# Eight PSUM banks as eight tiles instead of four pairs, in an attention and gated-product kernel on one core

## The chip, the cores and the metric

The kernel runs on one core of one Trainium2 chip. The metric is the device time of one execution in microseconds; lower is better. Three runs of the kernel before took 1008.64, 1010.52 and 1010.98 us, so the median is 1010.52 us.

## The reference

Windowed attention for 8 batches, 8 heads, 576 positions and head size 64 (four heads with a plain window of 32, four with a dilated one), and then a gated product on its output, all in float32:

```python
scores = scale * np.matmul(q, k.transpose(0, 1, 3, 2))
...
masks = np.stack([mask_plain if h < H // 2 else mask_dil for h in range(H)], axis=0)
scores = np.where(masks[None, :, :, :], scores, -1000000000.0)
scores = scores - np.max(scores, axis=-1, keepdims=True)
attn = np.exp(scores)
attn = attn / (np.sum(attn, axis=-1, keepdims=True) + 1e-09)
return np.matmul(attn, v).astype(np.float32)
...
g = x @ w_gate                      # x: 4608 x 512, w_gate and w_val: 512 x 1536
silu = g * (1.0 / (1.0 + np.exp(-g)))
val = x @ w_val
return (silu * val @ w_out).astype(np.float32)     # w_out: 1536 x 512
```

## The kernel before

The tokens are handled in nine chunks of 512. Attention is cut into "packs" of block-diagonal windows. For each pack TensorE writes scores into PSUM, VectorE subtracts the maximum, ScalarE takes the exponential, TensorE turns the result round and multiplies it by the values, and VectorE divides. Each float32 product of the second half is made of three matmuls of split operands (high by high, high by low, low by high), 128x512 each. The work comes in three stages.

**First packs.** Packs 0 to 3 run before any product, by an order written out by hand for TensorE, VectorE and ScalarE (the string of letters: Q scores, S shift, X exponential, T turn, K copy of the turned block, A results, N norm, G the first gate and value products, W stages that prepare weights).

**Plain chunks** (lines 880 to 912). Three chunks, twelve steps each, 36 steps s in all. A step makes twelve matmuls for the gate half g(s) into `bank_g` and twelve for the value half v(s) into `bank_v` (both line 485), and twelve output matmuls out(s-1) for the step before into the four banks `bank_o` (line 532). ScalarE takes the tanh of `bank_g` (line 504), VectorE multiplies it by `bank_g` (u, line 509) and by `bank_v` (h, line 514); ScalarE and GpSimd split h into high and low (lines 519 and 524), which out(s) reads. In program order a step is: g, tanh, u, v, h, out of the step before. VectorE also mixes weights for the third stage here (lines 696 to 709), and SyncE's queue writes them to memory as "pieces".

**Fast chunks** (lines 917 to 952). Three times two chunks at once, with seven products t = 0 to 6 in place of eight. In the gate part, for i = 0 to 5 and each t, `gate_val` makes six matmuls for r = 0 (gate) and six for r = 1 (value) (line 819). In the output part, for each t and i, `outs` makes three matmuls for r = 0 and three for r = 1. `BANK` says which pair of banks a t writes: 0 is `bank_g` and `bank_v`, 1 and 2 are the two pairs of `bank_o`; r picks the bank in the pair. After r = 0 or r = 1 of t = 0, 2 and 4 `keep` copies that bank to SBUF on ScalarE (line 824); after t = 1, 4, 5 and 6 `total` adds a bank and a kept copy on VectorE (line 780), in the gate part for both r after both products, in the output part (`out_done`) for each r right after its own product. Later products of the same pair add onto the bank, or start it afresh where t is in `FRESH`:

```python
BANK = (0, 1, 0, 2, 0, 1, 2)
FRESH = (0, 1, 3, 5)
KEPT = {0: 0, 2: 1, 4: 2}
SUMS = {1: ((0, 0), 1, 0), 4: ((1, 1), 2, 2), 5: ((1, 0), 1, 2), 6: ((0, 1), 2, 1)}
```

The weights' pieces come in through a ring of seven, each transfer asked for on GpSimd's queue (line 747) once TensorE has finished the piece whose place it takes.

PSUM has eight banks. Before, they are four tiles of two banks: `bgv` (gate and value), `two` (attention), `boa` and `bob` (outputs). The scores of the first packs use `bgv` and `boa`, their turned blocks the two halves of `bob`. Outside the hand-written part the order on each engine is set by a scheduler from the waits between tiles and its own estimate of durations; the waits themselves are put in by the framework from what each instruction reads and writes.

Of the kernel before, what the change touches and what calls it, by code (L numbers as in the profile page):

```python
# [10 lines left out]
F32 = mybir.dt.float32  # L11
# [7 lines left out]
P = 128  # L19
# [40 lines left out]
T0 = NPLAIN * CH  # L60
# [75 lines left out]
def attention_moe(ctx, tc, qkb, vb, w, const, out):  # L136
# [3 lines left out]
    def pk(m):  # L140
        return PACKS[m]
# [156 lines left out]
    def w_one(c):  # L298
        u = done[c]
        done[c] += 1  # L300
        if c == "E":
            w_exp(u)
        elif c == "T":
            w_shift(u)
        elif c == "B":
            w_bits(u)
        elif c == "H":
            w_split_hi(u)
        else:
            w_split_lo(u)  # L310
        if c in "BL":
            while ready["w"] and w_load():
                pass
# [22 lines left out]
    def load_qk(m, pool, engine, parts=1):  # L336
        t = pool["qk"]()
        n = pk(m).cols // parts
        for k in range(parts):
            engine.dma_start(out=t[:, n * k:n * k + n], in_=qkb[m, :, n * k:n * k + n])  # L340
        st[m]["qk"] = t
# [14 lines left out]
    def scores(m, two, masked):  # L356

        t = st[m]["qk"]
        if masked:
            for i in range(2):  # L360
                nc.tensor.matmul(out=two[:, i, SA:].rearrange("q (g k) -> q g k", g=NG), lhsT=ident16,
                                 rhs=masks_of(m, i), start=True, stop=False, skip_group_check=True)
        for g in range(NG):
            for j in range(NH):
                for i in range(2):
                    r, q, k = slice(D * i, D * i + D), pk(m).q_at(g, j), pk(m).k_at(i, g, j)
                    nc.tensor.matmul(out=two[BQ * j:BQ * j + BQ, i, SA + BU * g:SA + BU * g + BU],  # L367
                                     lhsT=t[r, q:q + BQ], rhs=t[r, k + 1:k + BK], start=not masked,
                                     stop=not masked or g == NG - 1, skip_group_check=True)

    def clear_e(pool):

        for a in pool["e"].starts:
            nc.gpsimd.memset(at(a, TP).rearrange("q (n k) -> q n k", k=BK)[:, :, :1], 0.0)

    def shift(m, two, pool, masked):
        mx = pool["bm"](2 * NG).rearrange("q (i g) -> q i g", i=2)
        e = pool["e"]()
        ev = e.rearrange("q (g i k) -> q i g k", g=NG, i=2)[:, :, :, 1:]
        s = two[:, :, SA:].rearrange("q i (g k) -> q i g k", g=NG)  # L380
        if not masked:
            n = BK * pk(m).mask
            if pk(m).mask_step:
                mk = mask_sb[:, n:n + 2 * BK * NG].rearrange("q (i g k) -> q i g k", i=2, g=NG)[:, :, :, 1:]
            else:
                mk = masks_of(m, 0).unsqueeze(1).broadcast_to([P, 2, NG, BU])
            nc.vector.tensor_tensor(out=ev, in0=s, in1=mk, op=ALU.add)
            s = ev
        nc.vector.reduce_max(out=mx, in_=s, axis=mybir.AxisListType.X)
        nc.vector.tensor_tensor(out=ev, in0=s, in1=mx.unsqueeze(3).broadcast_to([P, 2, NG, BU]), op=ALU.subtract)  # L390
        st[m]["e"] = e
# [5 lines left out]
    def turn_e(m, bank):  # L397
        for g in range(NG):
            nc.tensor.transpose(out=bank[:, P * g:P * g + P], in_=st[m]["e"][:, P * g:P * g + P], identity=eye)

    def keys(m, bank, pool):
        t = pool["pt"]()
        nc.scalar.copy(out=t, in_=bank)
        st[m]["pt"] = t

    def results(m, two):

        t, v = st[m]["pt"], st[m]["v"]
        for n in range(NH * NG):
            g, j = divmod(n, NH)  # L410
            for i in range(2):
                r = slice(D * i, D * i + D)
                nc.tensor.matmul(out=two[BQ * j:BQ * j + BQ, i, (D + 1) * g:(D + 1) * (g + 1)],
                                 lhsT=t[r, BQ * n:BQ * n + BQ], rhs=v[r, n, :], start=True, stop=True,
                                 skip_group_check=True)

    def norm(m, two, pool):
        z = pool["bz"](2 * NG).rearrange("q (i g) -> q i g", i=2)
        y = pool["y"]()
        s = two[:, :, :NG * (D + 1)].rearrange("q i (g c) -> q i g c", g=NG)  # L420
        nc.vector.tensor_scalar(out=z, in0=s[:, :, :, D], scalar1=EPS, scalar2=None, op0=ALU.add)
        nc.vector.reciprocal(out=z, in_=z)
        nc.vector.tensor_tensor(out=y.rearrange("q (c i g d) -> q i g c d", c=2, i=2, g=NG),  # L423
                                in0=s[:, :, :, :D].rearrange("q i g (c d) -> q i g c d", c=2),
                                in1=z.unsqueeze(3).unsqueeze(4).broadcast_to([P, 2, NG, 2, D // 2]), op=ALU.mult)
        st[m]["y"] = y
# [31 lines left out]
    def x_copy(m, what):  # L458
        src, xh, xl = x_views(m, *(t[pk(m).half % 2][pk(m).strided] for t in (x_hi, x_lo)))
        if what == "hi":  # L460
            nc.scalar.copy(out=xh, in_=src)
        else:
            nc.gpsimd.tensor_tensor(out=xl, in0=src, in1=xh, op=ALU.subtract)
# [17 lines left out]
    def gv_some(ci, f, which, ops, first, last):  # L481

        for n, (j, wl, xl) in enumerate(ops):
            o = 4 * P * (j // 2) + 2 * P * which + P * (j % 2)
            nc.tensor.matmul(out=(bank_g, bank_v)[which][:, :CH], lhsT=wcol(f, o, wl),  # L485
                             rhs=(x_lo if xl else x_hi)[ci % 2][1 - j // 2][:, j % 2],
                             start=first and n == 0, stop=last and n == len(ops) - 1)
# [3 lines left out]
    def gv_ops(text):  # L491

        return [(j, *PARTS[x]) for t in text.split() for x in t[1:] for j in ((2, 3) if t[0] == "p" else (0, 1))]
# [41 lines left out]
    def out_store(ci):  # L535
# [7 lines left out]


    fa = early
    bank_gv, two, bank_a, bank_b = [ctx.enter_context(tc.tile_pool(name="p" + x, bufs=1, space=bass.MemoryType.PSUM)).tile(
        [P, 2, 512], F32, name=x) for x in ("bgv", "two", "boa", "bob")]
    bank_g, bank_v = [bank_gv[:, n] for n in range(2)]
    bank_o = [x[:, n] for x in (bank_a, bank_b) for n in range(2)]
    s_banks, bank_r, k_bank = [bank_gv, bank_a], two, [bank_b[:, n % 2] for n in range(4)]  # L550

    nc.scalar.dma_start(out=const_sb, in_=const)
    load_qk(0, fa, nc.sync, 2)
# [28 lines left out]
    def more_in():  # L582
        load_v(3, fa, nc.sync, 2)
        w_load(2)
        w_load(2)
        w_load(2)
        ready["w"] = True
# [4 lines left out]
    first = {  # L592
        "Q": lambda m: scores(m, s_banks[m % 2], True), "S": lambda m: shift(m, s_banks[m % 2], fa, True),
        "X": exps, "T": lambda m: turn_e(m, k_bank[m]), "K": lambda m: keys(m, k_bank[m], fa),
        "A": lambda m: results(m, bank_r), "N": lambda m: norm(m, bank_r, fa),
        "U": turn_y, "H": lambda m: x_copy(m, "hi"), "L": lambda m: x_copy(m, "lo"),
        "M": lambda m: more_in(), "W": lambda n: w_one(STAGES[n]),
        "G": lambda n: gv_some(0, 0, first_gv[n][0], gv_ops(first_gv[n][1]), *first_gv[n][2:]),
    }

    et = mybir.EngineType
    with tc.manual_schedule(engines={et.PE, et.DVE, et.Activation}):
        for what in ("Q0 S0 Q1 X0 T0 S1 K0 X1 A0 M0 Q2 T1 K1 S2 N0 U0 X2 A1 W0 W1 W2 T2 K2 H0 L0 N1 W3 W4 U1 H1 L1 Q3 S3 A2 X3 N2 U2 "
                     "G0 W0 T3 K3 H2 L2 W1 W2 A3 W3 W4 N3 U3 G1 W0 W1 H3 L3 W2 G2 G3 G4 W3 G5 G6 W4 W0 W1 W2 W3 W4").split():
            first[what[0]](int(what[1]))
    load_qk(4, later, nc.sync)
    clear_e(later)
    while w_load():
# [252 lines left out]
    def n_out(ci, t, i):  # L861
        return NT * NP * ci + NP * t + i
# [54 lines left out]
    for ci in range(NC):  # L917
        base = SB + NSLOT * ci
        first = n_out(ci, 0, 0)
# [18 lines left out]
        for t in range(NT):  # L938
            for i in range(NP):
                n = n_out(ci, t, i)  # L940
# [57 lines left out]
```

## Time and profile before

| | |
|---|---|
| median of three runs | 1010.52 us |
| the profiled execution's own time | 1010.02 us |
| its span in the profile | 1008.2 us |
| TensorE (PE) busy | 940.2 us |
| weight loads (PEld) busy | 736.5 us |
| VectorE (DVE) busy | 663.4 us |
| ScalarE (ACT) busy | 391.0 us |
| GpSimd (POOL) busy | 363.6 us |
| mean granted TensorE clock | 0.977 |

The sum of a prediction is made against 1010.02 us, 1.8 us more than the span; the median of the runs is 0.5 us above that. In the rows, "PE" is a matmul, "PEld" the load of its weights; "idle before" or a bracket with an arrow names the work whose end released the instruction.

### The profile page before, as it was taken

The numbers are of one execution on the slowest core, as the hardware profiler recorded it, in microseconds if no ns is written. First come the engines' busy times: TensorE is split into PE (matmuls) and PEld (weight loads), VectorE is DVE, ScalarE is ACT, GpSimd is POOL, SyncE is SP. The second block draws the span as 40 slices with busy tenths as digits, with TensorE's granted clock in tenths as the row PEclk, the third lists the DMA queues.
The fourth block names the chain that finished last, engine by engine and source line by source line (L and its number), as shares of the span: only waits on it lengthen the run. The fifth ranks groups of instructions, "written<-read, shape, count | busy, mean of one in ns | idle before, by whom it ended". The sixth has DMA issues, their size and how long they took to land.

```text
span 1008.2 us, 20464 instructions
## 1 busy us (share of the span) xinstructions
PE 940.2 (93%) x8597; PEld 736.5 (73%) x8597; DVE 663.4 (66%) x966; ACT 391.0 (39%) x605; POOL 363.6 (36%) x369
## 2 busy tenths in 40 slices
PE   6799999999999999999999799999988999999988
PEld 3577776777777777777777587777766878877776
DVE  5466735676767786576679945767689745656933
ACT  3656532222233233333345343333344533333341
POOL 1555641212311221223334562232246733334562
PEclk7899999999999999999999899999999999999999
DMA  9556434565675792676685478777754676656562
GB/s 355 189 209 229 136 99 153 182 216 189 215 251 191 261 328 73 201 237 223 193 267 192 155 214 249 237 220 250 233 163 139 209 234 205 190 173 197 154 207 103
DMA packets 73964, 204.65 MB, mean 203 GB/s; under 512 B 7440, under 2 KB 21392, under 8 KB 73872
## 3 DMA queue, kind: packets, MB, share of 16 engines
q0 software_dynamic: 27216, 99.10, 32.4%
q1 hardware_dynamic: 36864, 66.43, 18.5%
q10 hardware_dynamic: 9792, 37.80, 11.1%
q8 instruction: 68, 1.11, 0.5%
q14 instruction: 24, 0.20, 0.1%
HBM read 160.84 MB, written 42.47 MB: 202 GB/s over the span
## 4 chain that ended last, share of the span: by engine, by line
PE 65%; DVE 23%; ACT 6%; issue 4%; DMA 1%; POOL 0%; ACTq 0%; SPq 0%; DVEq 0%
PE bgv L819 18%; PE bgv L485 14%; PE boa L819 12%; PE bob L819 12%; DVE at_float L780 5%; PE boa L532 3%; PE bob L532 3%; DVE at_float32r L780 2%; DVE at_float L847 2%; DVE at_float L848 1%; DVE at_float L509 1%; DVE at_float L423 1%; DVE at_float L696 1%; ACT at_float L504 1%; PE two L367 1%
## 5 line engine op out<-in xcount | busy, mean ns | idle before, releaser
L819 PE MATMUL bgv<-at_float32r 128*128 128x512 f32 x972 | 252.7, 400 | 14.1 <-ACT at_float L824 14.1
L485 PE MATMUL bgv<-at_float32r,at_float32r 128*128 128x512 f32 x864 | 222.1, 407 | 29.9 <-DVE at_float L509 17.8
L819 PEld LDWEIGHTS bgv<-at_float32r 128*128 128x128 f32 x972 | 178.6, 190 | 66.4 <-ACT at_float L824 30.7
L485 PEld LDWEIGHTS bgv<-at_float32r,at_float32r 128*128 128x128 f32 x864 | 162.1, 193 | 75.7 <-DVE at_float L509 26.7
L747 POOL DMA_DIRECT2D at_float32r<-pieces x189 | 103.2, 546 | 300.4 <-PE bgv L819 135.0
L819 PE MATMUL boa<-at_float32r 128*128 128x512 f32 x648 | 167.8, 399 | 10.4 <-DVE at_float L780 10.4
L819 PE MATMUL bob<-at_float32r 128*128 128x512 f32 x648 | 161.5, 394 | 1.3 <-DVE at_float L780 1.3
L819 PEld LDWEIGHTS boa<-at_float32r 128*128 128x128 f32 x648 | 123.3, 192 | 39.0 <-DVE at_float L780 12.5
L819 PEld LDWEIGHTS bob<-at_float32r 128*128 128x128 f32 x648 | 120.3, 188 | 29.1 <-DVE at_float L780 3.4
L780 DVE TENSOR_TENSOR at_float32r<-at_float,at_float32r 128x512 fp32r<-128x512 f32 (+1 forms) x84 | 88.2, 1058 | 55.8 <-ACT at_float32r L809 44.2
L524 POOL TENSOR_TENSOR at_float32r<-at_float,at_float32r 128x512 fp32r<-128x512 f32 x36 | 56.5, 1568 | 180.7 <-ACT at_float32r L519 87.9
L809 ACT CAST at_float32r<-at_float 128x512 fp32r<-128x512 f32 x126 | 76.2, 621 | 95.3 <-DVE at_float L780 27.4
L824 ACT COPY at_float<-bgv 128x512 f32<-128x512 f32 x126 | 73.9, 586 | 101.3 <-PE bgv L819 101.1
L780 POOL TENSOR_TENSOR at_float32r<-at_float,at_float32r 128x512 fp32r<-128x512 f32 x63 | 91.4, 1455 | 27.0 <-ACT at_float32r L809 26.2
L780 DVE TENSOR_TENSOR at_float<-bob,at_float 128x512 f32<-128x512 f32 x84 | 56.7, 685 | 59.7 <-ACT at_float L824 50.4
L845 ACT ACTIVATE at_float<-at_float 128x512 f32<-128x512 f32 x72 | 45.5, 632 | 99.6 <-DVE at_float L780 99.3
L780 DVE TENSOR_TENSOR at_float<-boa,at_float 128x512 f32<-128x512 f32 x84 | 54.7, 684 | 42.7 <-PE boa L819 41.8
L847 DVE SCALAR_TENSOR_TENSOR at_float<-at_float,at_float 128x512 f32<-128x512 f32 x72 | 57.5, 798 | 18.1 <-ACT at_float L845 16.4
L532 PE MATMUL bob<-at_float32r,at_float32r 128*128 128x512 f32 x216 | 65.1, 397 | 0.0
L509 DVE SCALAR_TENSOR_TENSOR at_float<-at_float,bgv 128x512 f32<-128x512 f32 x36 | 24.7, 686 | 60.9 <-ACT at_float L504 60.9
L780 POOL TENSOR_TENSOR at_float<-at_float,at_float 128x512 f32<-128x512 f32 x36 | 51.5, 1430 | 36.0 <-DVE at_float L848 30.8
L532 PE MATMUL boa<-at_float32r,at_float32r 128*128 128x512 f32 x216 | 64.0, 399 | 0.0
(74 smaller groups left out, 948.4 us busy)
## 6 DMA issues: line engine op xcount, KB each, us to landing
at_float32r<-pieces POOLq DMA_DIRECT2D x189, 512.0 KB, 4.3
pieces<-at_float32r SPq DMA_DIRECT2D x126, 256.0 KB, 3.8
at_float<-qkb ACTq DMA_DIRECT2D x31, 576.0 KB, 6.2
at_float<-vb ACTq DMA_DIRECT2D x34, 520.0 KB, 4.9
at_int<-w SPq DMA_DIRECT2D x19, 768.0 KB, 4.5
out<-at_float SPq DMA_DIRECT2D x36, 256.0 KB, 3.4
at_int<-w SPq DMA_DIRECT2D x10, 384.0 KB, 7.0
at_float<-qkb SPq DMA_DIRECT2D x8, 288.0 KB, 5.3
```

The lines of the kernel that those rows point to most:

```text
L367: nc.tensor.matmul(out=two[BQ * j:BQ * j + BQ, i, SA + BU * g:SA + BU * g + BU], lhsT=t[r, q:q + BQ], rhs=t[r, k + 1:k + BK], start=not ma ...
L485: nc.tensor.matmul(out=(bank_g, bank_v)[which][:, :CH], lhsT=wcol(f, o, wl), rhs=(x_lo if xl else x_hi)[ci % 2][1 - j // 2][:, j % 2], sta ...
L509: last["h"] = nc.vector.scalar_tensor_tensor(out=t, in0=t, scalar=1.0, in1=bank_g[:, :CH], op0=ALU.add, op1=ALU.mult)
L524: nc.gpsimd.tensor_tensor(out=hl, in0=hst[i][0], in1=hst[i][1], op=ALU.subtract)
L532: nc.tensor.matmul(out=bank_o[j][:, :CH], lhsT=wcol(f, 2 * DM + P * j, low), rhs=x, start=f == 0 and low == 0 and x is hh, stop=f == NF - ...
L747: nc.gpsimd.dma_start(out=taken[asked], in_=pieces[asked % NPIECE])
L780: engine.tensor_tensor(out=out, in0=a, in1=b, op=op)
L809: nc.scalar.copy(out=o[:, 0], in_=src)
L819: nc.tensor.matmul(out=bank, lhsT=w, rhs=x, start=first and n == 0 and t in FRESH, stop=last and n == len(ops) - 1, skip_group_check=True)
L824: nc.scalar.copy(out=kept[KEPT[t]][r], in_=banks[0][r][:, :CS])
L845: nc.scalar.activation(out=f, in_=g, func=AF.Tanh, scale=0.5)
L847: nc.vector.scalar_tensor_tensor(out=f, in0=f, scalar=1.0, in1=g, op0=ALU.add, op1=ALU.mult)
```

## The change

Each PSUM bank that holds products becomes a tile of its own. `two` stays a tile of two banks, in a pool at the left. The turned blocks of the first packs get two one-bank tiles `fk` and `fx` at the right side, the scores of the first packs two two-bank tiles `fs0` and `fs1` at the left. After the last use of the scores (S3) the pools of the scores are closed, and `bg`, `bv`, `bo0` and `bo1` are opened in their place, ahead of the first products; after the hand-written part the pools of the turned blocks are closed and `bo2` and `bo3` opened. The hand-written order is cut in two at that point, and its letters are the same. A pool opened with `reuse_waits="tile"` waits for the users of the tiles whose place it takes.

```diff
-    bank_gv, two, bank_a, bank_b = [ctx.enter_context(tc.tile_pool(name="p" + x, bufs=1, space=bass.MemoryType.PSUM)).tile(
-        [P, 2, 512], F32, name=x) for x in ("bgv", "two", "boa", "bob")]
-    bank_g, bank_v = [bank_gv[:, n] for n in range(2)]
-    bank_o = [x[:, n] for x in (bank_a, bank_b) for n in range(2)]
-    s_banks, bank_r, k_bank = [bank_gv, bank_a], two, [bank_b[:, n % 2] for n in range(4)]
+    of_scores, of_turns = ExitStack(), ExitStack()
+
+    def bank(stack, name, n, side="left"):
+        pool = stack.enter_context(tc.tile_pool(name="p" + name, bufs=1, space=bass.MemoryType.PSUM, side=side,
+                                                reuse_waits="tile"))
+        return pool.tile([P, 512] if n == 1 else [P, n, 512], F32, name=name)
+
+    two = bank_r = bank(ctx, "two", 2)
+    k_bank = [bank(of_turns, x, 1, "right") for x in ("fk", "fx")] * 2
+    s_banks = [bank(of_scores, x, 2) for x in ("fs0", "fs1")]
...
     with tc.manual_schedule(engines={et.PE, et.DVE, et.Activation}):
...
+        for what in "Q0 S0 Q1 X0 T0 S1 K0 X1 A0 M0 Q2 T1 K1 S2 N0 U0 X2 A1 W0 W1 W2 T2 K2 H0 L0 N1 W3 W4 U1 H1 L1 Q3 S3".split():
             first[what[0]](int(what[1]))
+        of_scores.close()
+        bank_g, bank_v, *bank_o = [bank(ctx, x, 1) for x in ("bg", "bv", "bo0", "bo1")]
...
+    of_turns.close()
+    bank_o += [bank(ctx, x, 1) for x in ("bo2", "bo3")]
```

No instruction is added or removed on any engine; the order of the engines' rows changes, on TensorE most of all. In the middle of a plain chunk TensorE's rows of one step stood like this before (the first twelve are g, the second twelve v; the output matmuls of the step before stand on both sides of v):

```order
L485 MATMUL bgv<-at_1024_float32r,at_1536_float32r 128x512 x12
L532 MATMUL boa<-at_512_float32r,at_1536_float32r 128x512 x4
L532 MATMUL bob<-at_512_float32r,at_1536_float32r 128x512 x3
L485 MATMUL bgv<-at_1024_float32r,at_1536_float32r 128x512 x12
L532 MATMUL bob<-at_512_float32r,at_1536_float32r 128x512
L532 MATMUL boa<-at_512_float32r,at_1536_float32r 128x512 x2
L532 MATMUL bob<-at_512_float32r,at_1536_float32r 128x512 x2
```

And now at the same place (`bo_446`, `bo_450`, `bo_583` and `bo_587` are the four output banks):

```order
L485 MATMUL bg<-at_1024_float32r,at_1536_float32r 128x512 x12
L485 MATMUL bv<-at_1024_float32r,at_1536_float32r 128x512 x12
L532 MATMUL bo_446<-at_512_float32r,at_1536_float32r 128x512 x2
L532 MATMUL bo_450<-at_512_float32r,at_1536_float32r 128x512 x2
L532 MATMUL bo_583<-at_512_float32r,at_1536_float32r 128x512 x2
L532 MATMUL bo_587<-at_512_float32r,at_1536_float32r 128x512 x2
L532 MATMUL bo_446<-at_512_float32r,at_1536_float32r 128x512
L532 MATMUL bo_450<-at_512_float32r,at_1536_float32r 128x512
L532 MATMUL bo_583<-at_512_float32r,at_1536_float32r 128x512
L532 MATMUL bo_587<-at_512_float32r,at_1536_float32r 128x512
```

The value half now follows the gate half at once, and the twelve output matmuls stand together behind it.

In the gate part of the fast chunks TensorE's rows stood like this before, here with their waits (an entry in brackets is the counter of a transfer queue or of an engine that the row waits for; Activation is ScalarE, DVE is VectorE):

```order
L819 MATMUL bgv<-at_1024_float32r 128x512 [waits DMASW6_49,Activation_49]
L819 MATMUL bgv<-at_1024_float32r 128x512 x5
L819 MATMUL bob<-at_1024_float32r 128x512 [waits DMASW7_49,DVE_49]
L819 MATMUL bob<-at_1024_float32r 128x512 x5
L819 MATMUL bgv<-at_1024_float32r 128x512 [waits Activation_49]
L819 MATMUL bgv<-at_1024_float32r 128x512 x5
L819 MATMUL bob<-at_1024_float32r 128x512 x6
L819 MATMUL bgv<-at_1024_float32r 128x512 [waits DMASW0_49,Activation_49]
```

And now, in the same part:

```order
L830 MATMUL bg<-at_1024_float32r 128x512 [waits DMASW3_49,Activation_49]
L830 MATMUL bg<-at_1024_float32r 128x512 x5
L413 MATMUL two<-at_1040_float_748,at_512_float_813 32x65 [waits DMAHW5_49,Activation_49]
L413 MATMUL two<-at_1040_float_748,at_512_float_813 32x65 x31
L367 MATMUL two<-at_1280_float_588 32x63 [waits DMAHW6_49]
L367 MATMUL two<-at_1280_float_588 32x63 x31
L830 MATMUL bv<-at_1024_float32r 128x512 x6
L830 MATMUL bo_446<-at_1024_float32r 128x512 [waits DMASW4_49,DVE_49]
L830 MATMUL bo_446<-at_1024_float32r 128x512 x5
L830 MATMUL bo_450<-at_1024_float32r 128x512 [waits DVE_49]
```

Before, the two halves of one t were parted by a half of the next t; now they stand in the order of the program, with an attention pack between them here, and the value half `bv` of this t waits for nothing.

SyncE's rows stand as before. On GpSimd 60 of 374 instructions stand at another place, by four places at most; on ScalarE 141 of 675, by four at most; on VectorE 210 of 968, twenty of them by more than three places and one by thirteen, where a gate part passes into an output part.

More of the change, by code (lines that the diff above doesn't have):

```diff
@@ L602, in attention_moe @@
     with tc.manual_schedule(engines={et.PE, et.DVE, et.Activation}):
-        for what in ("Q0 S0 Q1 X0 T0 S1 K0 X1 A0 M0 Q2 T1 K1 S2 N0 U0 X2 A1 W0 W1 W2 T2 K2 H0 L0 N1 W3 W4 U1 H1 L1 Q3 S3 A2 X3 N2 U2 "
-                     "G0 W0 T3 K3 H2 L2 W1 W2 A3 W3 W4 N3 U3 G1 W0 W1 H3 L3 W2 G2 G3 G4 W3 G5 G6 W4 W0 W1 W2 W3 W4").split():
+        for what in "Q0 S0 Q1 X0 T0 S1 K0 X1 A0 M0 Q2 T1 K1 S2 N0 U0 X2 A1 W0 W1 W2 T2 K2 H0 L0 N1 W3 W4 U1 H1 L1 Q3 S3".split():
             first[what[0]](int(what[1]))
+        of_scores.close()
+        bank_g, bank_v, *bank_o = [bank(ctx, x, 1) for x in ("bg", "bv", "bo0", "bo1")]
+        for what in ("A2 X3 N2 U2 G0 W0 T3 K3 H2 L2 W1 W2 A3 W3 W4 N3 U3 G1 W0 W1 H3 L3 W2 G2 G3 G4 W3 G5 G6 W4 "
+                     "W0 W1 W2 W3 W4").split():
+            first[what[0]](int(what[1]))
+    of_turns.close()
+    bank_o += [bank(ctx, x, 1) for x in ("bo2", "bo3")]
     load_qk(4, later, nc.sync)
```

## The prediction

> **What bounds the kernel now.** I read the page's busy shares first, then the waits of TensorE (PE) and of its weight loads (PEld), then the timeline at three of those waits.
>
> ```profile
> span 1008.2 us, 20464 instructions
> PE 940.2 (93%) x8597; PEld 736.5 (73%) x8597; DVE 663.4 (66%) x966; ACT 391.0 (39%) x605; POOL 363.6 (36%) x369
> PE 65%; DVE 23%; ACT 6%; issue 4%; DMA 1%; POOL 0%; ACTq 0%; SPq 0%; DVEq 0%
> ```
>
> TensorE is the bound: 93% busy, and 65% of the chain that ended last. But VectorE holds 23% of that chain, so TensorE waits for it somewhere. The waits say where; the columns are total us, times, longest.
>
> ```profile
> PE bgv L485 <- DVE at_float L509: 17.8, 15, 2.3
> PE bgv L819 <- ACT at_float L824: 14.1, 16, 2.6
> PE boa L819 <- DVE at_float L780: 10.4, 3, 6.4
> PE bgv L485 <- DVE at_float L514: 1.7, 2, 1.2
> PE bob L819 <- DVE at_float L780: 1.3, 2, 0.8
> ...
> PEld bgv L819 <- ACT at_float L824: 30.7, 63, 3.0
> PEld bgv L485 <- DVE at_float L509: 26.7, 31, 2.7
> PEld boa L819 <- DVE at_float L780: 12.5, 6, 6.8
> PEld bob L819 <- DVE at_float L780: 3.4, 6, 1.2
> PEld bgv L485 <- DVE at_float L514: 2.9, 5, 1.4
> ```
>
> Each of these is a write into a tile from which another engine still reads, and the counts say that it is the neighbour bank. Line 824 is `keep`: three kept t by six i by three passes is 54 in the gate parts and three by three is 9 in the output parts, where r = 1 follows a kept r = 0: 63, the number of loads that waited for line 824. Two places show the two banks apart; the columns are start, duration, engine, line.
>
> ```profile
> 328.51 2.62 PEld L485 LDWEIGHTS bgv<-at_float32r,at_float32r 128*128 128x128 f32 x12
> 328.52 3.04 PE L485 MATMUL bgv<-at_float32r,at_float32r 128*128 128x512 f32 x12
> 334.29 0.63 ACT L504 ACTIVATE at_float<-bgv 128x512 f32<-128x512 f32 x1
> 334.95 0.69 DVE L509 SCALAR_TENSOR_TENSOR at_float<-at_float,bgv 128x512 f32<-128x512 f32 x1 [0.32 <-ACT at_float L504]
> 335.69 4.05 PEld L485 LDWEIGHTS bgv<-at_float32r,at_float32r 128*128 128x128 f32 x12 [2.72 <-DVE at_float L509]
> 335.70 4.60 PE L485 MATMUL bgv<-at_float32r,at_float32r 128*128 128x512 f32 x12 [2.28 <-DVE at_float L509]
> ```
>
> The twelve at 328.52 are g, the twelve at 335.70 are v. Lines 504 and 509 read `bank_g` alone, v writes `bank_v` alone, and yet v starts 0.06 us after line 509 ends. So in the kernel before a tile of two banks is waited for as a whole. In the gate part it is the same with `keep`:
>
> ```profile
> 434.00 1.52 PE L819 MATMUL boa<-at_float32r 128*128 128x512 f32 x6
> 435.51 0.57 ACT L824 COPY at_float<-bgv 128x512 f32<-128x512 f32 x1
> 436.13 1.65 PE L819 MATMUL bgv<-at_float32r 128*128 128x512 f32 x6 [0.60 <-ACT at_float L824]
> ```
>
> The third kind, at a passage from gate to output part, is the longest wait of the trace:
>
> ```profile
> 568.18 0.68 DVE L780 TENSOR_TENSOR at_float<-boa,at_float 128x512 f32<-128x512 f32 x1
> 568.92 1.65 PE L819 MATMUL boa<-at_float32r 128*128 128x512 f32 x3 [6.38 <-DVE at_float L780]
> ```
>
> The last three matmuls of t = 1, r = 1 wait until `out_done` has read the bank of r = 0, for which VectorE, with other work ahead, comes late.
>
> **The change, term by term.** It adds and removes no instruction. It takes away the ties between neighbour banks, and with them the reason for the woven order. SyncE's queue keeps its order and GpSimd's transfers for pieces move past at most a few subtractions, so I cost both at nothing; what covers that is the ring of seven pieces.
>
> What a wait costs lies between two readings. The PE rows count idle time only after a matmul's modelled end: 17.8 + 1.7 + 14.1 + 10.4 + 1.3 = 45.3 us, the lower end. The PEld rows count from the end of the last load: 26.7 + 2.9 + 30.7 + 12.5 + 3.4 = 76.2 us in 31 + 5 + 63 + 6 + 6 = 111 waits. In the row of 328.51 twelve loads take 2.62 us; with the page's mean of 193 ns for one (below) they start (2.62 - 0.19) / 11 = 0.22 us apart, so 0.03 us between two loads is normal, and 111 of these are 3.3 us: 72.9 us, the upper end.
>
> ```profile
> L485 PEld LDWEIGHTS bgv<-at_float32r,at_float32r 128*128 128x128 f32 x864 | 162.1, 193 | 75.7 <-DVE at_float L509 26.7
> L780 DVE TENSOR_TENSOR at_float32r<-at_float,at_float32r 128x512 fp32r<-128x512 f32 (+1 forms) x84 | 88.2, 1058 | 55.8 <-ACT at_float32r L809 44.2
> ```
>
> I take the upper end: in the 335.70 case PE idles 2.28 us and PEld 2.72, and only loads and matmuls that start earlier shorten the kernel. The Trainium skill says the same of the two rows (Perfetto Trace Analysis, Identifying the Most-Contended Engine: matmul busy time is no good measure of what is left, since matmuls are pipelined; weight-load time is). By that rule the term is 72.9 us, by the PE rows 45.3.
>
> What of this comes back as a true wait? (1) g(s+1) truly needs u(s) to have read `bank_g`. Between them now stand v(s) and twelve output matmuls, 24 x 0.22 = 5.3 us. In the case shown, u ended at 335.64, 4.1 us after g's end (328.52 + 3.04); it would be covered. I take 2 us for later ones. (2) v(s+1) needs h(s), with the same 5.3 us, and out(s) needs its split, now 36 matmuls or 7.9 us after v(s): nothing. (3) t = 2 needs `keep` of t = 0, with 18 matmuls or 4.0 us between, more than the longest such wait of 3.0; only in the first i, where t = 2 comes right after t = 0, is it 6 matmuls or 1.3 us: nothing to 1 us, three times. (4) t = 6 needs `total` of t = 4, with 12 matmuls or 2.7 us between. Before, a half waited there for both reads, and all waits on `bob` are 3.4 us; I take 3 us back. (5) At the three passages VectorE is full:
>
> ```profile
> 540.00:560.00 20.00, 19.48 (x206) 15.48 (x205) 20.00 (x27) 8.40 (x14) 10.68 (x10) 1.00 0.60 190
> 320.00:340.00 20.00, 17.09 (x190) 13.02 (x189) 15.23 (x26) 7.39 (x10) 1.46 (x1) 0.91 0.62 210
> 560.00:580.00 20.00, 13.62 (x54) 10.66 (x53) 18.61 (x18) 8.41 (x15) 10.64 (x11) 0.83 0.54 175
> 740.00:760.00 20.00, 17.39 (x192) 13.39 (x191) 17.07 (x25) 7.81 (x14) 5.56 (x8) 0.91 0.59 183
> 760.00:780.00 20.00, 17.17 (x127) 13.10 (x125) 18.67 (x24) 10.07 (x16) 16.46 (x11) 0.91 0.39 112
> 960.00:980.00 20.00, 19.13 (x77) 15.48 (x78) 6.59 (x9) 8.68 (x15) 12.30 (x14) 0.91 0.64 188
> ```
>
> (Columns: stretch, PE, PEld, DVE, ACT, POOL busy, then the granted clock.) From 540 to 560 us VectorE is busy 20.00 of 20. The splits of h that the output part reads run eight (t, i) ahead, 8 x 6 matmuls or 10.6 us, so TensorE can pass a VectorE that is 6.4 us late, but not by much more. Of the 12.5 us on `boa` I give back half, 6 us. Sum of (1) to (5): 2 + 1 + 3 + 6 = 12 us. Net: 72.9 - 12 = 61 us.
>
> The clock is a term of its own. In the five stretches above with 0.91 or 0.83 it is below 1, which costs 4 x 0.09 x 20 + 0.17 x 20 = 10.6 us. Each holds a TensorE wait of over 2 us that should go: the 2.28 and 6.38 us shown, and these three:
>
> ```profile
> 748.65 2.16 PE L819 MATMUL bgv<-at_float32r 128*128 128x512 f32 x6 [2.03 <-ACT at_float L824]
> 769.41 1.14 PE L819 MATMUL bgv<-at_float32r 128*128 128x512 f32 x3 [2.60 <-ACT at_float L824]
> 960.87 1.38 PE L819 MATMUL boa<-at_float32r 128*128 128x512 f32 x3 [2.63 <-DVE at_float L780]
> ```
>
> The bounds are 0 and 10.6 us; I take 5, since three of the five lie where VectorE is full. The Trainium skill (TensorE: Matmul & The Clock Gate, Part 1) lets the clock fall to half only after an idle window of about 3.4 us. By that rule only the wait of 6.38 us would cost clock, and the term would be at most the 3.4 us of 560 to 580; the trace differs, since waits of 2.0 to 2.6 us have a low clock beside them too.
>
> Sum against the profiled execution's own 1010.0 us: 1010 - 61 - 5 = 944 us. The median of the runs is 0.5 us above it, so 945.
>
> **Rivals.** *VectorE takes over.* With TensorE some 6% ahead, VectorE's 663 us of work stand in fewer microseconds, and where it shares time with GpSimd one split takes 1.06 us on average (the row of line 780) against 0.68 for the read of `boa` above. The price: all 15.9 us of the waits on `boa` and `bob` come back, the clock's 5 us are not won, and of the 57.4 us on lines 509 and 824 a third turns into true waits, 19 us. Gain 72.9 - 16 - 19 = 38 us: 972. For it speaks VectorE's 20.00 of 20; against it the 66% over the whole span.
>
> *The ties stay and only their cover goes.* The woven order put 7 output matmuls between g and v, and a half of another t before a kept t's second half. If the wait for the neighbour were still in force, by the reuse of pools or by an engine's counter that holds more than the one read, each v would stand behind tanh and u at the bare price of 0.63 + 0.69 = 1.3 us (35 times, 46 us), each of 63 halves behind a copy of 0.57 + 0.06 (40 us) and nine output halves behind 0.68 (6 us): 92 us against the 72.9 paid now. VectorE's lateness adds the cover that is lost: 7 x 0.22 = 1.5 us on each of the 31 v that waited already, 48 us. That is 19 to 67 us slower, 1053 in the middle. It decides from the point where v(s) must wait for u(s) at all. Against it: in the new rows the second half `bv` after a kept `bg` has no wait on ScalarE.
>
> *Nothing changes.* If something else held TensorE anyway (the pieces, the preparation of weights), the waits would only change their names: 1010, within 0.3% (3 us, about what runs of this kernel can tell apart). Against it: none of the waits shown is for a transfer.
>
> **How the numbers follow.** The forecast of 945 gets 0.70, with 930 to 960 as its own range: 72.9 and the clock's whole 10.6 us with nothing given back would be 927, and 45.3 us with 5 of clock would be 960. VectorE takes over (960 to 985) gets 0.19, no change 0.05, ties that stay 0.06. Faster is 0.70 + 0.19 = 0.89, same 0.05, slower 0.06. The range is 928 to 975: it leaves out the two last cases and the far end of VectorE's.
>
> **What would show it.** In the profile after, the waits of line 485 on line 509 and of line 819's successor on `keep` should nearly vanish as PEld rows (under 5 us each from 26.7 and 30.7), TensorE's busy time should stay near 900 to 940 us with a span of some 943, and the clock be 1.00 in the stretches that answer to 565, 750, 770 and 960 us. Waits on line 514, or on line 780's `total`, of over 20 us would show VectorE taking over. Rows of v that still start right behind line 509 would show the ties in force. The prediction is wrong if TensorE's waits go and the span doesn't follow, since then they were no part of the bound.

## The result, and the profile after

The changed kernel takes 950.35 us (median of four runs, 948.66 to 951.01) against 1010.75 us before: a ratio of 0.940, 95% interval 0.938 to 0.942. The forecast was 945, its own range 930 to 960. The profiled execution took 951.01 us, 59.0 us less than the one before.

The busy shares and the chain that ended last, from the page:

```profile
span 949.2 us, 20492 instructions
PE 914.9 (96%) x8597; PEld 739.6 (78%) x8597; DVE 659.1 (69%) x966; ACT 388.1 (41%) x605; POOL 358.0 (38%) x369
PE 78%; DVE 9%; DMA 3%; issue 3%; ACT 3%; POOL 2%; SPq 1%; ACTq 0%; POOLq 0%; DVEq 0%
```

The profile counts 28 instructions more than before (20492 against 20464), all of them for semaphores; the counts of the busy ones are the same. TensorE is more of the chain (78% from 65%), VectorE less (9% from 23%). The load time, 739.6 us, is 3.1 us above what it was: TensorE has the same work and waits less. The waits of its loads (total us, times, longest):

```profile
PEld two L399 <- ACT at_float L395: 9.6, 8, 3.5
PEld bo L830 <- DVE at_float32r L791: 5.9, 3, 2.7
...
PEld bg L485 <- DVE at_float L509: 3.9, 1, 3.9
...
PEld two L367 <- DMA at_float<-qkb: 1.9, 1, 1.9
...
PEld bg L830 <- DVE at_float32r L791: 1.7, 2, 1.2
...
PEld bg L830 <- POOL at_float32r L791: 0.8, 1, 0.8
PEld bo L830 <- DVE at_float L791: 0.7, 1, 0.7
```

(Lines 819, 824 and 780 of before are 830, 835 and 791 here.) No load of a product waits for `keep` any more (30.7 us before), the one that waits for line 509 stands in the first packs, and of the waits for a total 0.7 us is left. What is new are the splits of line 791 (5.9 + 1.7 + 0.8 = 8.4 us) and more on line 395 (9.6 from 5.6).

A plain step in the timeline (start, duration, engine, line):

```profile
299.63 3.02 PE L485 MATMUL bg<-at_float32r,at_float32r 128*128 128x512 f32 x12
302.48 2.89 PE L485 MATMUL bv<-at_float32r,at_float32r 128*128 128x512 f32 x12
303.13 0.59 ACT L504 ACTIVATE at_float<-bg 128x512 f32<-128x512 f32 x1
304.48 0.68 DVE L509 SCALAR_TENSOR_TENSOR at_float<-at_float,bg 128x512 f32<-128x512 f32 x1
```

The value half starts at 302.48 and is at work while the tanh (303.13) and u (304.48) still read `bg`. Before, such a row started 0.06 us after u had ended.

TensorE and its loads over the first 60 us and over the rest, of before and then of after (stretch, PE, PEld, DVE, ACT, POOL busy, granted clock, share of the transfer engines, GB/s):

```profile
0.00:60.00 60.00, 41.14 (x691) 28.68 (x692) 32.31 (x52) 30.87 (x43) 21.64 (x20) 0.83 0.73 264
60.00:1008.00 948.00, 899.03 (x7907) 707.77 (x7907) 631.05 (x915) 360.11 (x562) 341.98 (x349) 0.99 0.62 199
```

```profile
0.00:60.00 60.00, 43.61 (x700) 31.39 (x701) 33.32 (x54) 32.98 (x46) 21.61 (x20) 0.80 0.74 264
60.00:949.00 889.00, 871.29 (x7898) 708.22 (x7896) 625.79 (x913) 355.14 (x560) 336.35 (x349) 1.00 0.66 212
```

After 60 us the loads idle 948 - 707.8 = 240.2 us before and 889 - 708.2 = 180.8 after: 59.4 us less, for a busy time that is the same within 0.5. The matmuls' rows have idle times of 49.0 and 17.7: only 31.3 us less, and their busy time fell by 28 us without one matmul being left out.

### The profile page after: what moved, and what is told of

Its sections match the earlier page's. It is cut to its first block, busy times and chain, and to the rows that moved or that the text cites. A ratio compares the mean times of both kernels' runs of the same rounds, so it can differ in the third digit from the quotient of the medians.

```text
span 949.2 us, 20492 instructions
## 1 busy us (share of the span) xinstructions
PE 914.9 (96%) x8597; PEld 739.6 (78%) x8597; DVE 659.1 (69%) x966; ACT 388.1 (41%) x605; POOL 358.0 (38%) x369
## 4 chain that ended last, share of the span: by engine, by line
PE 78%; DVE 9%; DMA 3%; issue 3%; ACT 3%; POOL 2%; SPq 1%; ACTq 0%; POOLq 0%; DVEq 0%
PE bo L830 27%; PE bg L830 10%; PE bv L830 10%; PE bv L485 9%; PE bo L532 8%; PE bg L485 8%; DVE at_float L791 3%; PE two L413 2%; DVE at_float32r L791 2%; PE two L367 2%; DMA at_int<-w 2%; PE two L399 1%; POOL at_float32r L791 1%; DMA pieces<-at_float32r 1%; DMA at_float<-qkb 1%
## 5 line engine op out<-in xcount | busy, mean ns | idle before, releaser
L830 PE MATMUL bo<-at_float32r 128*128 128x512 f32 x1296 | 311.3, 393 | 4.9 <-DVE at_float32r L791 4.6
L830 PEld LDWEIGHTS bo<-at_float32r 128*128 128x128 f32 x1296 | 242.0, 188 | 58.0 <-DVE at_float32r L791 5.9
L791 DVE TENSOR_TENSOR at_float<-bo,at_float 128x512 f32<-128x512 f32 x168 | 113.4, 686 | 99.9 <-ACT at_float L835 53.5
L830 PE MATMUL bg<-at_float32r 128*128 128x512 f32 x486 | 130.6, 394 | 1.2 <-DVE at_float32r L791 0.8
L830 PE MATMUL bv<-at_float32r 128*128 128x512 f32 x486 | 128.9, 391 | 0.0
L485 PE MATMUL bg<-at_float32r,at_float32r 128*128 128x512 f32 x432 | 110.7, 405 | 8.7 <-issue 3.8
L485 PE MATMUL bv<-at_float32r,at_float32r 128*128 128x512 f32 x432 | 108.0, 398 | 0.8 <-ACT at_float32r L281 0.8
L830 PEld LDWEIGHTS bg<-at_float32r 128*128 128x128 f32 x486 | 90.8, 189 | 21.6 <-DVE at_float32r L791 1.7
L532 PE MATMUL bo<-at_float32r,at_float32r 128*128 128x512 f32 x432 | 107.4, 397 | 0.0
L830 PEld LDWEIGHTS bv<-at_float32r 128*128 128x128 f32 x486 | 90.8, 188 | 19.4
```

The source lines that it names most:

```text
L532: nc.tensor.matmul(out=bank_o[j][:, :CH], lhsT=wcol(f, 2 * DM + P * j, low), rhs=x, start=f == 0 and low == 0 and x is hh, stop=f == NF - ...
L791: engine.tensor_tensor(out=out, in0=a, in1=b, op=op)
L830: nc.tensor.matmul(out=bank, lhsT=w, rhs=x, start=first and n == 0 and t in FRESH, stop=last and n == len(ops) - 1, skip_group_check=True)
```

## The experiments

Two theories stood at the start. A: the time was in the waits for a neighbour bank, and any order in which these are gone is as fast. B: the time was in the woven order of TensorE's rows, and the straight order would be as fast with the old tiles. They differ on a kernel that has the straight order and the old tiles.

**The straight order, with the ties and without.** Two kernels put TensorE's rows of the plain and fast chunks in the order in which the program is written, the one on the tiles of before, the other on those of after:

```diff
-    for s in range(NS):
+    with tc.manual_schedule(engines={et.PE}):
+        for s in range(NS):
...
```

With the tiles of before:

> Tiles as before (pairs of banks), but TensorE's instructions of the main loops kept in written order: g, v, out of the step before, and both halves of a t one after the other, which is the order of the changed kernel to four instructions. Theory A (the wait for the neighbour bank is what cost time; the woven order only hid part of it): slower than before, 1030 to 1077 us by the bare prices of the prediction's second rival, with about 35 waits of v on line 509 and 63 on keep. Theory B (the straight order itself, fewer changes of bank and better cover, made the gain): 945 to 960 us.

With the tiles of after:

> Tiles of the changed kernel and the same written order on TensorE as in the run beside it; the two kernels differ in the tiles alone. Both theories: the changed kernel's time, 947 to 953 us, since its own order differs from the written one in four instructions. Control for the tied kernel.

With the ties it takes 1110.93 us, a ratio to before of 1.0995 (1.0956 to 1.1034); without them 952.49 us, 0.9415 (0.9389 to 0.9442). With the ties, from its waits and its timeline:

```profile
PEld bgv L819 <- ACT at_float L824: 76.8, 62, 4.4
PEld bgv L485 <- DVE at_float L509: 66.6, 35, 4.3
PEld boa L819 <- DVE at_float L780: 16.1, 6, 5.6
...
PEld bob L819 <- DVE at_float L780: 5.6, 4, 1.8
```

```profile
107.16 2.88 PE L485 MATMUL bgv<-at_float32r,at_float32r 128*128 128x512 f32 x12
110.14 0.60 ACT L504 ACTIVATE at_float<-bgv 128x512 f32<-128x512 f32 x1 [1.63 <-PE bgv L485]
110.78 0.69 DVE L509 SCALAR_TENSOR_TENSOR at_float<-at_float,bgv 128x512 f32<-128x512 f32 x1 [4.74 <-ACT at_float L504]
111.52 2.61 PEld L485 LDWEIGHTS bgv<-at_float32r,at_float32r 128*128 128x128 f32 x12 [0.22 <-DVE at_float L509]
111.52 3.04 PE L485 MATMUL bgv<-at_float32r,at_float32r 128*128 128x512 f32 x12
```

Thirty-five v, one for each step behind the first, wait for u, and 62 halves wait for `keep`. In the five rows the value half stands directly behind tanh and u of the bank beside it. So B falls: the straight order alone costs 100 us, and on single banks it takes 2.1 us more than after. Of A, it is shown that the ties cost the time, though A priced the tied kernel too low (1030 to 1077 us). That any order without them is as fast is not shown: the written order is nearly that of after, and the woven order was not run on single banks. Why the price was too low, the gate part of the tied kernel shows:

```profile
455.82 1.34 PEld L819 LDWEIGHTS bgv<-at_float32r 128*128 128x128 f32 x6
456.04 1.54 PE L819 MATMUL bgv<-at_float32r 128*128 128x512 f32 x6
457.62 0.59 ACT L824 COPY at_float<-bgv 128x512 f32<-128x512 f32 x1 [2.77 <-PE bgv L819]
458.25 1.23 PEld L819 LDWEIGHTS bgv<-at_float32r 128*128 128x128 f32 x6 [1.10 <-ACT at_float L824]
```

The last load ends at 457.16 and the last matmul at 457.58; the copy takes from 457.62 to 458.21. The bare price is 1.10 us: 0.42 for the matmul that is still running, 0.59 for the copy, 0.09 between them. The prediction's price had counted the copy alone, 0.63.

**One pair at a time.** In the first of these `bg` and `bv` are single banks and the outputs stay pairs, in the second it is the other way round, and in the third all stay pairs and only the pools of the first packs are as in after:

```diff
-        bank_g, bank_v, *bank_o = [bank(ctx, x, 1) for x in ("bg", "bv", "bo0", "bo1")]
+        bank_g, bank_v = [bank(ctx, x, 1) for x in ("bg", "bv")]       # first
+        bank_a = bank(ctx, "boa", 2)
+        bank_o = [bank_a[:, n] for n in range(2)]
...
+        bank_gv = bank(ctx, "bgv", 2)                                  # second
+        bank_g, bank_v = [bank_gv[:, n] for n in range(2)]
+        bank_o = [bank(ctx, x, 1) for x in ("bo0", "bo1")]
```

Single gate and value banks:

> Only the pair of the gate and value banks is parted; the four output banks stay two tiles of two. TensorE's order is that of the changed kernel. Theory A, by the terms of the prediction: the waits on lines 509, 514 and on keep go (60.3 us of weight-load rows), those of out_done between r = 0 and r = 1 stay (15.9 us and some clock): 955 to 968 us. Theory B (the order): no difference from the changed kernel, 950.

Single output banks:

> Only the four output banks are parted; gate and value stay one tile of two. Theory A: the waits of v on line 509 (26.7) and on keep (30.7) stay, the 15.9 us of out_done go with part of the clock: 990 to 1000 us. Theory B: between before and the changed kernel, in proportion to the rows that moved, about 970.

The pools of the first packs alone:

> Only the first packs' part of the change: scores and turned blocks in pools of their own at two sides, given back ahead of the first products; the products' banks are pairs as before. The order on every engine is that of before. Theory A (all of the gain is the products' banks): within 0.3% of before, 1008 to 1012 us, the first TensorE product at 25 us as before. Rival (the first packs' pools carry part of it): 1005 us or less.

They took 970.88 us, 0.9606 (0.9585 to 0.9626), 2.9 us above the expected range; 996.71 us, 0.9865 (0.9839 to 0.989); and 1010.77 us, 1.0012 (0.9999 to 1.0026). The new place of the first packs' pools is worth nothing that these runs can tell. The gate and value banks alone are worth 40.1 us against the 1010.96 us of before, run beside them, the output banks alone 14.3; together 54, and after has 60. Some 6 us are missing, and the waits show what one tie does when the other is gone. In the kernel with single gate and value banks, whose rows on TensorE stand as in after, the waits that are left, their longest in the timeline, and the stretches around the two longest:

```profile
PEld boa L833 <- DVE at_float L794: 20.1, 6, 8.2
...
PEld bob L833 <- DVE at_float L794: 6.2, 7, 2.2
```

```profile
743.88 1.65 PE L833 MATMUL boa<-at_float32r 128*128 128x512 f32 x3 [7.78 <-DVE at_float L794]
```

```profile
538.00:548.00 10.00, 7.24 (x23) 5.84 (x24) 9.43 (x9) 3.28 (x6) 5.58 (x5) 0.66 0.36 107
735.00:750.00 15.00, 7.22 (x20) 5.38 (x20) 14.46 (x15) 6.62 (x10) 7.68 (x6) 0.66 0.39 122
```

(Its line 794 is line 780 of before.) The six waits on `boa` rise from 12.5 to 20.1 us, those on `bob` from 3.4 to 6.2: 10.4 us more. That TensorE now comes to them earlier and VectorE does not is the likely reason, but was not tried by itself. The clock beside them falls to 0.66. Over these 25 us that would be 8.5 us, but much of the slow time lies in the waits themselves, where it costs nothing: at half clock TensorE works 4.33 us in the first stretch and 6.01 us in the second, which costs 5.2 us. In the mirror kernel the ties on `bgv` are 27.5 and 27.3 us, near what they were:

```profile
PEld bgv L485 <- DVE at_float L509: 27.5, 32, 2.7
PEld bgv L832 <- ACT at_float L837: 27.3, 65, 3.7
```

**What is left at the passages.** Behind the first packs, the longest waits of after on VectorE and on ScalarE, with the rows ahead of them:

```profile
545.13 4.68 DVE L791 TENSOR_TENSOR at_float<-at_float,at_float 128x1024 f32<-128x1024 f32 x2
...
549.73 3.55 DVE L791 TENSOR_TENSOR at_float32r<-at_float,at_float32r 128x512 fp32r<-128x512 f32 x4
551.53 1.77 PEld L830 LDWEIGHTS bo<-at_float32r 128*128 128x128 f32 x5 [2.72 <-DVE at_float32r L791]
```

```profile
102.94 0.90 ACT L239 ACTIVATE at_int<-at_int 128x768 f32<-128x768 f32 x1 [2.54 <-DMA at_int<-w]
103.72 0.63 ACT L395 ACTIVATE at_float<-at_float 128x504 f32<-128x504 f32 x1
...
104.40 0.72 PEld L399 LDWEIGHTS two<-at_bfloat,at_float 128*128 128x128 f32 x4 [3.53 <-ACT at_float L395]
```

In the first, two differences of 128x1024 for the next chunks (`x_step`) stand on VectorE ahead of the splits for which TensorE waits. In the second, an exponential that the turn of a pack needs stands on ScalarE behind a row that waits 2.54 us for weights. If these waits count, moving these x steps behind the output totals, and turning these packs one visit later, must each give their waits back; if VectorE's load as a whole had become the bound, neither would. The edits:

```diff
-    X_SLOTS = {88: 0, 92: 1, 96: 2, 99: 3, 102: 4, 105: 5, 108: 6, 111: 7, 124: 10}
+    X_SLOTS = {100: 0, 103: 1, 106: 2, 109: 3, 112: 4, 115: 5, 118: 6, 121: 7, 124: 10}
...
-                    x_step(X_SLOTS[slot])
+                    with tc.issue_after(last["o"].ins):      # the last output total
+                        x_step(X_SLOTS[slot])
```

```diff
-        visits(4 + n, a, a + 3, a + 2)
+        visits(4 + n, a, a + 4, a + 2)
```

The x steps later:

> The changed kernel, with the x splits and differences for the next two chunks asked for 12 to 15 places later in the output part and put behind the second read of t = 1, so that VectorE doesn't do them between the splits of h at the passage. Theory C (the part of the forecast that didn't come, about 6 us, is VectorE full at the passages): the loads' waits on the splits of line 791 fall from 8.4 us to under 3, and the time to 942 to 947. Rival D (VectorE is late there by its splits and GpSimd's share of its time, whatever else stands between): waits of 6 us or more, 948 to 952.

The turns later:

> The changed kernel, with the turning of the exponentials of packs 4 to 8 a third of a step later. Theory C' (the 9.6 us of loads that wait for line 395, up from 5.6 before, are a turn that stands too early on TensorE; one of 3.5 us at 101 us, with a low clock behind it, is in the first chunk): 2 to 5 us less, 945 to 948. Rival: the wait moves to the results (line 413) or the next scores: within 2 us of the changed kernel.

Both:

> Both of the last two edits. If each stands alone, their gains add: 938 to 944 us. If neither wins, 948 to 953.

They took 941.84 us, 0.9338 (0.9317 to 0.9358); 946.01 us, 0.9376 (0.9358 to 0.9395); and 938.35 us, 0.9295 (0.9276 to 0.9314). The last is the best of this study, 12 us below after, and the interval lies wholly below that of after. (After was not run again beside these; the before run beside them took 1009.04 us and not 1010.75, so by the ratios the three gains are 6.4, 2.5 and 10.7 us and not 8.5, 4.3 and 12.) With the x steps later, the waits for the splits fall from 8.4 us to the first row below; with both, TensorE is 97% busy, and the waits on line 395 are the second:

```profile
PEld bg L830 <- DVE at_float32r L791: 0.8, 2, 0.5
```

```profile
PEld two L399 <- ACT at_float L395: 5.7, 7, 1.4
```

The x steps alone gave 8.5 us by the medians. The waits on the splits fell by 7.6, and the clock that was low from 540 to 560 us (the stretches below) had cost 1.8; together these are somewhat more than was gained. The turns alone gave 4.3 us, while their row only went from 9.6 to 9.0 us in total and from 3.5 to 2.1 for the longest; 1.7 us of that is the clock from 100 to 110 us, and the intervals of that kernel and of after overlap, so for this part alone the size stays open.

## Why the prediction was right, and where not

**The waits, upper reading (72.9 us).** It held. Of the 76.2 us of load waits on lines 509, 514, 824 and 780, 4.6 us are left, and 3.9 of these stand at 41 us, in the first packs, where before stood a wait of 4.65 us for which the trace names no releaser. The matmuls' rows would have given 45.3 us; the kernel gained 59.0 with all that came back taken off. The rule quoted there (the Trainium skill, Perfetto Trace Analysis, Identifying the Most-Contended Engine) is borne out: the loads' busy time after 60 us stayed within 0.5 us, so their idle time fell by the whole gain, 59.4 us, where the matmuls' fell by 31.3. The tied kernel's rows at 456 us say why: a wait for a result begins when the last load is done, and the 0.42 us that the last matmul still runs count as busy in the one row and as idle in the other. Over 111 waits that is 47 us at most, where the two readings were 31 apart (76.2 and 45.3).

**What comes back (12 us).** The sum was near, its parts were not. (1), 2 us for g behind u, is nothing after 60 us. (3), 1 us, is nothing. (4), 3 us for t = 6, is at most the 0.7 us that is left on line 791's totals. (5), 6 us at the passages, is 8.4 us: TensorE meets a late VectorE there, as said, but it waits for the splits, and for the most part because of two differences that stand ahead of them, since the waits fell to 0.8 us once the x steps were moved. Two terms were not seen: 4.0 us more on line 395, of which 3.5 is the one wait shown, behind a ScalarE row that waits for weights, and 1.9 us for a transfer of `qkb`. That makes 0.7 + 8.4 + 4.0 + 1.9 = 15.0 against 12.

**The clock (5 us).** The size held, the bound and some places did not. The stretches of after that answer to those of before, and the one that was new:

```profile
100.00:110.00 10.00, 6.89 (x26) 5.39 (x25) 6.09 (x6) 6.05 (x9) 4.10 (x4) 0.83 0.36 128
320.00:340.00 20.00, 18.10 (x323) 14.27 (x322) 14.76 (x25) 5.93 (x8) 4.68 (x6) 1.00 0.98 332
540.00:560.00 20.00, 16.56 (x65) 12.90 (x64) 15.20 (x14) 8.64 (x16) 14.56 (x15) 0.91 0.71 222
740.00:760.00 20.00, 18.48 (x80) 14.80 (x80) 19.93 (x19) 12.80 (x23) 15.78 (x16) 1.00 0.70 211
900.00:920.00 20.00, 20.00 (x89) 16.42 (x88) 20.00 (x16) 11.81 (x21) 17.89 (x18) 1.00 0.81 261
```

Counted as the prediction counted, before's five stretches cost 10.6 us, and after's two cost 0.17 x 10 + 0.09 x 20 = 3.5 us, behind the waits of 3.53 and 2.72 us. In the three others it is 1.00, as forecast, but the one from 540 to 560 us, which answers to 565 us before, keeps a low clock, against the forecast. That count is too high where TensorE itself stands still: before, the half clock at 565 us lasts 6.82 us, and TensorE works in only 3.16 of them, which costs 1.6 us and not 3.4. The bound was therefore 8.4 us and not 10.6, and these stretches won 8.4 - 3.4 = 5.0 us. Around the first packs before has two slow times of 3.41 us with TensorE at work, from 43.02 and from 60.09 us; after has one, from 39.58 us, with 5.30 us of work: 0.8 us more won. The sum of the terms is then 72.9 - 15.0 + 5.0 + 0.8 = 63.7 us against 59.0 measured. Of the 4.7 us that are over, 3.5 are the spacing of the loads: their gaps of at most 60 ns, which are no rows of the waits, sum to 130.4 us after the first 60 us of the old kernel and to 137.2 us in the new one, 6.8 more, where the prediction took off 3.3. The rest stays without a name.

The stretches also bear on the page's idle window of about 3.4 us (the Trainium skill, TensorE: Matmul & The Clock Gate, Part 1). By that rule the loads' wait of 3.53 us would cost clock and the one of 2.72 us would not, and on the matmuls' rows, 3.11 and 2.30 us, neither would; both did. With the x steps later the second wait and its low clock are both gone, with the turns later the first (stretches of these two kernels, in this order):

```profile
540.00:560.00 20.00, 20.00 (x89) 16.43 (x88) 17.50 (x13) 13.55 (x24) 13.68 (x15) 1.00 0.68 204
```

```profile
100.00:110.00 10.00, 8.75 (x101) 6.76 (x102) 6.22 (x7) 6.52 (x10) 4.46 (x3) 1.00 0.27 94
```

**VectorE takes over (0.19).** Not in after, but its mechanism was seen in the kernel with single gate and value banks and tied outputs (970.88 us; that this is near the 972 of the rival is chance, since the waits on lines 509 and 824 did not come back): there the waits on `boa` and `bob` come back with more than they had. In after they don't, since the read for which they waited is of another bank.

**The ties stay and only their cover goes (19 to 67 us slower).** The tied kernel made that case, and it cost 100 us. What was mis-sized are the bare prices: a kept half costs 1.10 us and not 0.63 (62 waits averaging 76.8 / 62 = 1.24), and a value half 66.6 / 35 = 1.90 and not 1.3. With the outputs' 21.7 us the rows sum to 165 us where 76 stood before, 89 more of the 106 us by which the profiled execution is longer (1115.99 against 1010.02). The granted clock, 0.962 on average against 0.977, makes up to 19 us over the two spans, which would cover the rest. The counts, 35 and 62, were nearly as priced (35 and 63).

**No change (0.05).** Refuted: the waits did not merely change their names. That it was the pools of the first packs is refuted too, at 1010.77 us.

## What to carry to other kernels

Ask of each wait whether it is for the data or only for the tile that holds them: if two engines' rows touch different banks of one tile and still stand end to start, a tile per bank removes the wait, and no order woven to hide it is needed (here the straight one takes 952 us). Price such a wait by the idle time of the weight loads; the matmuls' row hides the end of the last matmul, here 0.42 us each. After one tie has been cut, look for the next one at once: in this kernel, single gate and value banks alone made the outputs' waits grow from 15.9 to 26.3 us.

## What the runs showed of the hardware

The granted clock falls beside waits that are shorter than I had expected to matter, and it costs as much as part of the wait. In the best kernel a wait of 2.33 us for a transfer is followed by twelve matmuls that take 4.61 us, where the same twelve took 2.89 us at 302.48 in after:

```profile
331.58 0.69 PEld L367 LDWEIGHTS two<-at_float 64*32 64x32 f32 x64 [2.33 <-DMA at_float<-qkb]
...
332.37 4.61 PE L485 MATMUL bv<-at_float32r,at_float32r 128*128 128x512 f32 x12
```

So a wait of 2.3 us cost 4.0 us there. The clock records of the ten traces show how that comes about. The granted clock is only ever 1 or 0.5 there, and it changes only on a grid of 3.41 us, so a slow time lasts 3.41 us or a whole multiple, and costs half of what TensorE works in it: 1.7 us. A stretch of 20 us at 0.91 holds one such time. What counts is how long TensorE idles within one step of the grid. Two steps of after around its wait of 2.30 us (matmul row), and two of the kernel with single output banks around one of 2.92 us:

```profile
548.17:551.58 3.41, 1.11 (x6) 0.61 (x4) 3.41 (x3) 0.76 (x2) 2.74 (x3) 1.00 1.04 323
551.58:555.00 3.42, 3.42 (x8) 2.77 (x9) 2.31 (x4) 0.62 (x1) 0.57 (x1) 0.50 0.18 66
```

```profile
565.97:569.39 3.42, 1.79 (x8) 1.14 (x7) 3.42 (x3) 3.04 (x6) 3.38 (x5) 1.00 0.85 270
569.39:572.80 3.41, 2.12 (x9) 1.67 (x10) 3.41 (x5) 0.59 (x1) 2.50 (x3) 1.00 0.92 208
```

The first wait lies in one step, which idles 2.30 us, and the next step runs at half clock. The second, longer wait is shared by two steps, which idle 1.63 and 1.29 us, and no slow time follows. Behind the first 62 us of the ten traces, 36 steps at full clock are followed by a slow one, and the matmuls' rows idle 1.82 us or more in each of them; in the 2581 that are not, they idle 1.88 us at most. So in these kernels some 1.85 us of idle time within one step cost the next step half its clock.
